# New offsets in the time table of a fused attention and MLP kernel

## Chip, cores and metric

The kernel runs on one core of one Trainium2 chip. The metric is the device time of one execution in microseconds; below that is 1107.98 us, the median of three runs (1107.72 to 1108.46).

## The reference

```python
qn = q / (np.linalg.norm(q, axis=1, keepdims=True) + 1e-06)      # q, k, v: (2, 6016, 256)
kn = k / (np.linalg.norm(k, axis=1, keepdims=True) + 1e-06)
s = kn.transpose(0, 2, 1) @ qn / tau
s = s - s.max(-1, keepdims=True)
a = np.exp(s)
a /= a.sum(-1, keepdims=True) + 1e-09
x = (v @ a).reshape(12032, 256)
h = x @ w_in                                                       # (256, 2048)
g = np.maximum(h, 0.0) + alpha * np.minimum(h, 0.0)
return g @ w_out                                                   # (2048, 256)
```

For each of two batches a 256 x 256 attention matrix is made over channels. It is multiplied into v, and the result goes through a two-layer MLP of hidden width 2048 with a leaky activation of a slope per hidden unit.

## The kernel before

The attention matrix and the first weight matrix are multiplied together once per batch (the blocks M), so the long part is only v @ M, the activation, and a product with w_out. The tokens are cut into 24 tiles (12 per batch) of 504 or 500, and the hidden width into eight pairs of 128, so there are 192 items, numbered tile x 8 + pair. All products are done in three passes of split fp32r operands (a high and a low part; `passes`, L486 to L488). Each item's first product is done as seven small block products in place of eight, so that TensorE saves an eighth and VectorE and ScalarE add and copy more.

The stages of an item i, each a planned step:

- `pe_a` (TensorE): two block products into bank q (six matmuls of half a tile's width). `copies` (ScalarE, L1015, L1016): they are copied into the accumulators r and into p7.
- `pe_b` (two products), then the *sum* `add_p7(i, 0)` (VectorE, L1032): r0 + p7 is written into bank r1. `pe_c` (two products) may come only behind it, since it adds to both. Then the second sum `add_p7(i, 1)`, and behind it `pe_d` (one product).
- `act_n` (ScalarE, L1045) multiplies by the slope, and the *maximum* `dve_g` (VectorE, L1054) makes g out of r and that. Both exist for fi = 0 and 1. The maximum of fi = 1 reads bank r1. In most tiles the next item has the same bank r1, so `add_p7(i+1, 0)` must wait until `dve_g(i, 1)` has finished reading it, though both run on VectorE.
- g is split by `g_high` (ScalarE, L1063) and `g_low` (VectorE, L1067), and `s2_first` and `s2_second` (TensorE) multiply by w_out into banks X. In 18 of the tiles, for four or six items of eight, the second product is done with seven blocks as well. There `g_sums` (VectorE, L1126, three chained differences into t), `x_high`, `x_low`, `t_high` (ScalarE, L1154) and `t_low` take the place of `g_high` and `g_low`. `t_low` is an ACTIVATE on ScalarE (L1148, the negative of a high part) and then an *adding transfer* that GpSimd issues (L1149), a DMA that adds t to it in place. `s2_second` of the item needs it from its second matmul on. The tiles g and t share a ring of four buffers, so a late adding transfer also holds back a later `act_n`.
- Per tile, `combine` and `finish_out` (L1230, L1236, L1242) put the output together and store it. `v_sums`, `v_high` and `v_low` prepare the next tile of v (L701, L719, L727). Behind `v_low(t, 0)` SP issues the load of the tile after it (`load_v`, L683), since there is one buffer. In the first batch `load_T` (L754) reads q and k once more for the norms of the second batch.

The first 92 us are written out by hand: the scores of batch 0, its softmax, and M. From there on all 4,051 steps come from a plan. Each has a slot (5.0 apart, one per item), a place within the slot from `ORDER` or a similar table, and an offset from `MOVED`, by stretch and slot. The sum of the three is its time, and the steps are issued in the order of these times. So only the order counts, and each engine's queue gets its steps in that order. The stretches are "first" (slots 0 to 20), "early" (from 21, and from 80; its eight offsets repeat per tile), "soft" (from 66), "m1" (from 90), "late" (from 108; repeats per tile for ten tiles) and "last" (from 188). For "early" the places are those of "sums" in slots whose item minus 2 takes the seven-block form (pe_b 2.29, s2 1.53 and 4.71, add 3.9, dve_g 4.3 and 2.85, g_sums 0.02, 0.2 and 2.04), and else those of "none" (pe_a 0.3, pe_c 0.7). In slot i stand pe_a, copies, pe_b and the first sum of item i, but pe_c, the second sum, pe_d, act_n and dve_g of item i - 1, and x, t and g parts of item i - 2.

```python
key = stretch(i) + (f.__name__ + "_".join(str(a) for a in args[1:]),)
time = i * PERIOD + at + MOVED.get(key[:2], {}).get(key[2], 0.0)
plan.append((time, len(plan), key, f, args))
...
for _, _, _, f, args in sorted(plan, key=lambda x: x[:2]):
    f(*args)
```

Of the kernel before, what the change touches and what calls it, by code (L numbers as in the profile page):

```python
# [79 lines left out]
    ("first", 3): dict(act_n0=-1.0, act_n1=-0.1, add_p70=1.5, add_p71=0.77, conv_b=0.8,  # L80
        copies=0.57, dve_g0=2.73, dve_g1=5.09, g_high0=0.59, g_high1=1.18, g_low0=4.24,
        g_low1=4.96, pe_a=-2.37, pe_b=0.2, pe_c=-0.27, pe_d=-0.64, pe_fill=1.89, pe_s2=-0.69,
        split_wo=2.74),
    ("first", 4): dict(act_n0=1.1, act_n1=0.17, add_p70=-0.93, add_p71=1.05, copies=0.47,
        dve_g0=1.01, dve_g1=0.84, g_high0=1.33, g_high1=2.64, g_low0=1.1, g_low1=2.99,
        pe_a=-2.16, pe_b=-1.38, pe_c=0.93, pe_d=-0.11, pe_s2=-0.28, split_wo=-2.54, v_high1=7.05,
        v_sums0=-3.0, v_sums1=0.98),
    ("first", 5): dict(act_n0=0.04, act_n1=4.41, add_p70=-0.69, add_p71=-0.69, copies=-0.77,
        dve_g0=-0.01, dve_g1=5.92, g_high1=-1.47, g_low0=2.1, g_low1=-1.59, load_T0=-2.8,
        load_T1=-3.28, load_T2=6.67, pe_a=-3.81, pe_b=-1.96, pe_c=-1.52, pe_d=-2.56, pe_s2=-1.46,  # L90
        square_T0=-2.45, square_T1=1.36, square_T2=2.03, v_high0=-2.49, v_high2=2.11),
    ("first", 6): dict(act_n0=0.21, act_n1=0.07, add_p70=0.12, copies=0.8, dve_g0=0.5,
        dve_g1=0.91, g_high0=-0.8, g_high1=2.49, g_low0=-0.85, g_low1=3.36, pe_a=-1.75,
        pe_b=-1.15, pe_c=-2.65, pe_d=-1.8, pe_s2=-0.69, v_low0=-0.41),
    ("first", 7): dict(act_n0=-1.63, act_n1=-1.7, add_p70=0.18, add_p71=-0.75, copies=-0.74,
        dve_g0=-1.2, dve_g1=-0.39, g_high0=-1.05, g_high1=-2.52, g_low0=-0.12, g_low1=-3.0,
        pe_a=-1.61, pe_b=-0.72, pe_c=-0.92, pe_d=-2.05, pe_s2=-0.73, v_low1=3.87, v_low2=-3.11),
    ("first", 8): dict(act_n0=-0.48, act_n1=2.35, add_p70=0.17, add_p71=-0.17, copies=2.22,
        dve_g0=-0.3, dve_g1=1.48, evac=6.09, g_high0=3.97, g_high1=-3.21, g_low0=3.66,
        g_low1=-0.62, pe_a=-2.57, pe_b=0.46, pe_c=-1.18, pe_d=0.57, pe_s2=-0.51),  # L100
    ("first", 9): dict(act_n0=-2.31, act_n1=0.63, add_p70=-0.18, add_p71=-0.38, copies=1.48,
        dve_g0=0.96, dve_g1=0.54, g_high0=-0.89, g_high1=-0.37, g_low0=0.56, g_low1=-2.28,
        pe_a=-0.57, pe_b=0.03, pe_c=-1.85, pe_d=-2.31, pe_s2=-0.91, s_weights0=-13.67,
        s_weights1=-3.96, s_weights2=-3.42, s_weights3=-8.36, s_weights4=4.64, v_sums0=-2.21,
        v_sums1=4.9),
    ("first", 10): dict(act_n0=0.1, act_n1=2.33, add_p70=0.54, add_p71=1.08, copies=0.84,
        dve_g0=0.18, dve_g1=1.73, g_high0=3.94, g_high1=-0.61, g_low0=3.4, g_low1=-2.19,
        pe_a=-1.46, pe_b=-0.91, pe_c=-1.87, pe_d=0.88, pe_s2=0.27, s_weights0=-10.6,
        s_weights1=-0.09, s_weights2=1.29, s_weights3=-1.45, s_weights4=3.57,
        s_weights_high=4.86, v_high0=-3.62, v_high1=2.17, v_high2=0.26),  # L110
    ("first", 11): dict(act_n0=0.59, act_n1=0.06, add_p70=1.28, add_p71=-0.62, copies=0.7,
        dve_g0=0.7, dve_g1=1.33, g_high0=6.9, g_high1=1.24, g_low0=6.07, g_low1=-1.19, pe_a=0.06,
        pe_b=1.9, pe_c=-1.26, pe_d=-1.73, s2_first=-3.59, s_weights0=-5.95, s_weights1=-2.47,
        s_weights2=-0.94, s_weights3=-4.51, s_weights4=5.66, s_weights_high=3.08,
        s_weights_low=6.86),
    ("first", 12): dict(act_n0=-0.09, act_n1=1.67, add_p70=-0.11, add_p71=-0.12, copies=0.32,
        dve_g0=0.6, dve_g1=0.85, g_high0=5.03, g_high1=0.44, g_low0=5.09, g_low1=3.0, pe_a=-0.2,
# [1485 lines left out]
```

## Time and profile before

| | |
|---|---|
| median of three runs | 1107.98 us |
| profiled execution | 1108.53 us, its span 1106.8 us |
| TensorE busy | 1098.9 us (99%) |
| weight loads busy | 1026.3 us (93%) |
| VectorE, ScalarE busy | 967.8 us (87%), 904.0 us (82%) |
| GpSimd busy | 127.5 us (12%) |

TensorE's matmuls and its weight loads have rows of their own (PE and PEld). A load normally runs under the matmul ahead of it. A matmul that must wait for a semaphore holds its load back as well, so such waits stand with PEld. DVE is VectorE, ACT ScalarE, POOL GpSimd, SP the queue of most loads and stores.

### The profile page before, as it was taken

Reading aid. Unit: us, or ns where it says so; the run is one execution under the profiler, and the core shown is the slowest. Engines: PE = TensorE matmul, PEld = TensorE weight load, DVE = VectorE, ACT = ScalarE, POOL = GpSimd, SP = SyncE. Lnnn points to the kernel's source line nnn. Section 1 sums busy time; section 2 is a strip of 40 time slices with the busy share of each in tenths; the row PEclk is TensorE's granted clock in tenths of the full one; section 3 lists DMA queues with packets and bytes.
Section 4 is the critical chain, followed back from the end, with each engine's and each line's share of the span. In section 5 each row is a group of like instructions: output and inputs, shape, how many; then the busy total and the mean of one; then the engine's idle time right before and its main releaser. Section 6 shows DMA issues by size and latency. Waiting matters only on the chain.

```text
span 1106.8 us, 20835 instructions
## 1 busy us (share of the span) xinstructions
PE 1098.9 (99%) x7752; PEld 1026.3 (93%) x7752; DVE 967.8 (87%) x1853; ACT 904.0 (82%) x1553; POOL 127.5 (12%) x156
## 2 busy tenths in 40 slices
PE   9999999999999999999999999999999999999998
PEld 8888888999999899899999989999999999999997
DVE  6798898888888888988988988999999999999975
ACT  6797777888888789777777778889889889888965
POOL 0000000011011011011000001121211122112100
PEclk9999999999999999999999999999999999999999
DMA  9997322545545545123431207557667666666520
GB/s 329 374 332 277 79 74 73 138 113 124 136 114 124 131 113 130 38 74 76 94 97 46 63 8 157 121 116 147 132 116 139 130 126 131 129 128 131 112 57 19
DMA packets 68661, 139.69 MB, mean 126 GB/s; under 512 B 6224, under 2 KB 37200, under 8 KB 68432
## 3 DMA queue, kind: packets, MB, share of 16 engines
q0 software_dynamic: 31040, 64.15, 31.1%
q1 hardware_dynamic: 37520, 74.21, 19.7%
q8 instruction: 61, 1.00, 0.4%
q14 instruction: 40, 0.33, 0.1%
HBM read 59.78 MB, written 14.42 MB: 67 GB/s over the span
## 4 chain that ended last, share of the span: by engine, by line
PE 94%; DMA 2%; DVE 2%; ACT 1%; issue 0%; SPq 0%; ACTq 0%; DVEq 0%
PE X L486 13%; PE X L487 13%; PE X L488 13%; PE r L486 11%; PE r L488 10%; PE r L487 10%; PE S L788 7%; PE o L1270 4%; PE q L488 4%; PE q L486 4%; PE q L487 4%; DMA tgl<-t 1%; PE pm L940 1%; DVE g L1054 1%; ACT g L1045 0%; DMA kqs<-q_dram 0%
## 5 line engine op out<-in xcount | busy, mean ns | idle before, releaser
L1054 DVE SCALAR_TENSOR_TENSOR g<-r,sgn,g 128x500 f32<-128x500 f32 (+1 forms) x384 | 280.4, 735 | 44.9 <-ACT g L1045 42.3
L1045 ACT ACTIVATE g<-r,salpha 128x500 f32<-128x500 f32 (+1 forms) x384 | 258.3, 681 | 58.3 <-DVE r L1032 19.9
L486 PE MATMUL r<-vs,m 128*128 128x250 f32 (+1 forms) x960 | 276.1, 288 | 2.0 <-DVE r L1032 1.6
L487 PE MATMUL r<-vs,m 128*128 128x250 f32 (+1 forms) x960 | 268.1, 279 | 0.0
L488 PE MATMUL r<-vs,m 128*128 128x250 f32 (+1 forms) x960 | 268.1, 279 | 0.0
L486 PEld LDWEIGHTS r<-vs,m 128*128 128x128 f32 x960 | 180.8, 188 | 20.2 <-DVE r L1032 8.3
L1032 DVE TENSOR_TENSOR r<-r,p 128x250 f32<-128x250 f32 (+1 forms) x384 | 162.5, 423 | 41.3 <-PE r L488 26.2
L487 PEld LDWEIGHTS r<-vs,m 128*128 128x128 f32 x960 | 181.3, 189 | 6.0
L488 PEld LDWEIGHTS r<-vs,m 128*128 128x128 f32 x960 | 181.6, 189 | 0.0
L1015 ACT COPY r<-q 128x500 f32<-128x500 f32 (+1 forms) x192 | 109.1, 568 | 76.0 <-DVE g L1054 43.9
L1149 POOL DMA_DIRECT2D tgl<-t x92 | 79.2, 861 | 572.9 <-ACT tgl L1148 422.0
L1067 DVE TENSOR_TENSOR gl<-g,gh 128x500 fp32r<-128x500 f32 (+1 forms) x200 | 133.0, 673 | 13.7 <-ACT gh L1063 13.5
L1063 ACT CAST gh<-g 128x500 fp32r<-128x500 f32 (+1 forms) x200 | 120.1, 613 | 27.7 <-DVE g L1054 24.5
L486 PE MATMUL X<-gh,wo 128*128 128x500 f32 (+1 forms) x336 | 131.6, 392 | 0.0
L487 PE MATMUL X<-gl,wo 128*128 128x500 f32 (+1 forms) x336 | 131.4, 391 | 0.0
L488 PE MATMUL X<-gh,wo 128*128 128x500 f32 (+1 forms) x336 | 131.2, 391 | 0.0
L486 PE MATMUL q<-vs,m 128*128 128x250 f32 (+1 forms) x384 | 107.6, 280 | 0.0
L488 PE MATMUL q<-vs,m 128*128 128x250 f32 (+1 forms) x384 | 107.2, 279 | 0.0
L487 PE MATMUL q<-vs,m 128*128 128x250 f32 (+1 forms) x384 | 107.2, 279 | 0.0
L1148 ACT ACTIVATE tgl<-t 128x1000 fp32r<-128x1000 f32 (+1 forms) x92 | 95.7, 1040 | 0.8 <-DVE t L1126 0.7
L1154 ACT CAST tgh<-t 128x1000 fp32r<-128x1000 f32 (+1 forms) x92 | 94.1, 1035 | 0.0
L1135 DVE TENSOR_TENSOR xl<-g,xh 128x750 fp32r<-128x750 f32 (+1 forms) x92 | 85.8, 932 | 0.0
(142 smaller groups left out, 2443.0 us busy)
## 6 DMA issues: line engine op xcount, KB each, us to landing
tgl<-t POOLq DMA_DIRECT2D x66, 500.0 KB, 4.6
tgl<-t POOLq DMA_DIRECT2D x26, 504.0 KB, 4.6
kqT<-kqT_dram SPq DMA_DIRECT2D x20, 512.0 KB, 3.7
kq<-k_dram SPq DMA_DIRECT2D x39, 256.0 KB, 5.4
kq<-q_dram SPq DMA_DIRECT2D x39, 256.0 KB, 5.4
...
```

The source lines that it names most:

```text
L486: nc.tensor.matmul(out, wh, xh, start=first, stop=False, **s)
L487: nc.tensor.matmul(out, wh, xl, start=False, stop=False, **s)
L488: nc.tensor.matmul(out, wl, xh, start=False, stop=last, **s)
L1015: nc.scalar.copy(r_t[i][0][:, :, :h], x[:, 0:1, :h].broadcast_to([P, 2, h]))
L1032: nc.vector.tensor_tensor(out=r[1][:, n, :h], in0=r[0][:, 1, :h], in1=p7_t[i][:, :h], op=ALU.add)
L1045: nc.scalar.activation(blocks(g_t[i], i, 2 * fi, 2 * fi + 2), r_t[i][fi][:, :, : half_of(i)], AF.Copy, scale=salpha[:, f : f + 1],)
L1054: nc.vector.scalar_tensor_tensor(out=g, in0=r_t[i][fi][:, :, : half_of(i)], scalar=sgn[:, f : f + 1], in1=g, op0=ALU.mult, op1=ALU.max,)
L1063: nc.scalar.copy(gs_t[i][0][:, fi, :w], g_t[i][:, fi * w : fi * w + w])
L1067: nc.vector.tensor_tensor(out=gs_t[i][1][:, fi, :w], in0=g_t[i][:, fi * w : fi * w + w], in1=f32(gs_t[i][0][:, fi, :w]), op=ALU.subtract,)
L1135: nc.vector.tensor_tensor(out=xs_t[i][1][:, h : 4 * h], in0=g_t[i][:, h : 4 * h], in1=f32(xs_t[i][0][:, h : 4 * h]), op=ALU.subtract,)
L1148: nc.scalar.activation(ts_t[i][1][:, :w], tt_t[i][:, :w], AF.Copy, scale=-1.0)
L1154: nc.scalar.copy(ts_t[i][0][:, :w], tt_t[i][:, :w])
```

## The change

Only the table `MOVED` is changed: nearly all offsets are new. No step is added or left out, no function, tile size, buffer or bank differs. On VectorE 1,156 of 1,700 instructions of the plan stand in another place of its queue, on ScalarE 864 of 1,410, on TensorE 454 of 1,169 steps, on GpSimd 9 of 148, on SP 5 of 100.

```diff
 MOVED = {
...
-    ("early", 0): dict(act_n0=-0.19, act_n1=0.14, add_p70=-1.0, add_p71=-0.14, copies=-0.55,
-        dve_g0=-1.09, dve_g1=-0.24, g_sums0=0.76, g_sums1=0.6, g_sums2=0.36, pe_a=0.4,
-        pe_b=-0.09, pe_c=0.06, pe_d=-1.12, s2_first=0.49, s2_second=-0.76, t_high=1.32,
-        t_low=2.24, v_sums0=-2.11, x_high=0.25, x_low=1.13),
+    ("early", 0): dict(act_n0=-0.21, act_n1=-0.06, add_p70=-0.43, add_p71=0.67, copies=-0.29,
+        dve_g0=-0.9, dve_g1=-0.28, g_sums0=1.59, g_sums1=2.36, g_sums2=0.86, pe_a=-0.5,
+        pe_b=-0.1, pe_c=0.07, pe_d=-1.43, s2_first=0.89, s2_second=-0.75, t_high=-1.04,
+        t_low=1.81, v_sums0=0.77, x_high=0.41, x_low=2.76),
...
-    ("early", 2): dict(act_n0=0.66, act_n1=1.6, add_p70=0.2, add_p71=1.78, combine0=-1.74,
-        combine1=-0.73, combine2=0.7, combine_copy=-1.56, copies=-1.77, dve_g0=0.82, dve_g1=0.82,
-        g_sums0=-1.84, g_sums1=1.24, g_sums2=1.04, pe_a=-2.26, pe_b=1.3, pe_c=-1.18, pe_d=-0.3,
-        s2_first=-1.92, s2_second=0.61, t_high=0.15, t_low=0.91, v_high0=-11.47, x_high=1.03,
-        x_low=4.51),
-    ("early", 3): dict(act_n0=-3.17, act_n1=0.05, add_p70=0.19, add_p71=-0.19, copies=0.41,
-        dve_g0=-0.4, dve_g1=0.24, finish_out0=0.68, finish_out1=0.9, g_high0=0.48, g_high1=2.6,
-        g_low0=0.46, g_low1=5.94, pe_a=-0.28, pe_b=-2.1, pe_c=-0.3, pe_d=-1.88, s2_first=0.38,
-        s2_second=-0.52),
-    ("early", 4): dict(act_n0=1.74, act_n1=-0.03, add_p70=0.44, add_p71=0.46, copies=-2.13,
-        dve_g0=1.14, dve_g1=0.95, g_sums0=-1.05, g_sums1=0.11, g_sums2=0.29, pe_a=-3.12,
-        pe_b=1.45, pe_c=-1.19, pe_d=0.65, s2_first=0.29, s2_second=-1.66, t_low=2.8, v_low0=0.31,
-        x_high=0.39, x_low=2.3),
+    ("early", 2): dict(act_n0=1.15, act_n1=0.52, add_p70=0.56, add_p71=0.47, combine0=0.16,
+        combine1=0.21, combine2=0.49, combine_copy=-0.13, copies=0.3, dve_g0=0.29, dve_g1=0.87,
+        g_sums0=-1.3, g_sums1=1.19, g_sums2=0.7, pe_a=-2.0, pe_b=1.18, pe_c=-2.05, pe_d=0.36,
+        s2_first=-0.27, s2_second=-0.87, t_high=-0.07, t_low=2.97, v_high0=-10.75, x_high=1.01,
+        x_low=2.55),
+    ("early", 3): dict(act_n0=-1.76, act_n1=0.18, add_p70=-0.56, add_p71=-0.28, copies=0.43,
+        dve_g0=-1.17, dve_g1=0.21, finish_out0=-0.66, finish_out1=-0.78, g_high0=0.3,
+        g_high1=0.07, g_low0=8.08, g_low1=5.25, pe_a=-0.81, pe_b=-1.43, pe_c=-1.13, pe_d=-1.65,
+        s2_first=-1.33, s2_second=-0.48),
+    ("early", 4): dict(act_n0=2.88, act_n1=1.1, add_p70=-0.55, add_p71=-1.43, copies=1.24,
+        dve_g0=1.8, dve_g1=0.17, g_sums0=-1.14, g_sums1=2.85, g_sums2=1.5, pe_a=-1.6, pe_b=0.58,
+        pe_c=-1.82, pe_d=2.75, s2_first=2.62, s2_second=-2.61, t_high=-1.55, t_low=3.47,
+        v_low0=3.42, x_high=-1.02, x_low=4.54),
...
-        load_T0=-0.91, load_T1=-2.11, load_T2=1.54, pe_a=-1.54, pe_b=-0.83, pe_c=-0.7, pe_d=0.38,
+        load_T0=-2.31, load_T1=3.68, load_T2=1.61, pe_a=-0.25, pe_b=-0.7, pe_c=0.16, pe_d=-0.47,
...
-    ("late", 0): dict(act_n0=0.12, act_n1=1.46, add_p71=0.83, copies=0.55, dve_g0=-0.3,
-        dve_g1=0.97, g_sums0=1.27, g_sums1=1.1, g_sums2=0.01, pe_a=-3.1, pe_b=1.52, pe_c=-0.47,
-        pe_d=-0.54, s2_first=-3.25, s2_second=2.69, t_high=-3.55, t_low=0.55, v_sums0=-4.53,
-        x_high=1.21, x_low=-0.28),
+    ("late", 0): dict(act_n0=0.01, act_n1=1.46, add_p70=0.29, add_p71=-0.75, copies=0.94,
+        dve_g0=-0.12, dve_g1=1.25, g_sums0=1.14, g_sums1=1.06, g_sums2=-0.66, pe_a=-1.78,
+        pe_b=0.56, pe_c=-0.77, pe_d=-0.29, s2_first=-4.77, s2_second=2.23, t_high=-4.33,
+        t_low=0.61, v_sums0=-5.14, x_high=1.78, x_low=1.88),
...
-    ("late", 3): dict(act_n0=-0.14, act_n1=-0.31, add_p70=0.03, add_p71=0.26, copies=-0.22,
-        dve_g0=-0.08, dve_g1=0.65, finish_out0=1.11, finish_out1=0.1, g_high0=1.02,
-        g_high1=-0.82, g_low0=2.17, g_low1=-1.4, g_sums0=0.36, g_sums1=2.3, g_sums2=1.05,
-        pe_a=-1.08, pe_b=0.01, pe_c=-1.1, pe_d=-0.92, pe_s2=0.8, s2_first=-2.29, s2_second=-1.74,
-        t_high=-0.16, t_low=1.03, x_high=2.18, x_low=1.88),
+    ("late", 3): dict(act_n0=-0.96, act_n1=0.04, add_p70=0.27, add_p71=0.28, copies=-1.87,
+        dve_g0=-0.13, dve_g1=0.03, finish_out0=-0.63, finish_out1=-0.25, g_high0=-1.36,
+        g_high1=-0.88, g_low0=-0.47, g_low1=2.26, g_sums0=-0.44, g_sums1=0.42, g_sums2=-0.06,
+        pe_a=-2.49, pe_b=-0.07, pe_c=-0.66, pe_d=-1.57, pe_s2=-0.83, s2_first=-0.38,
+        s2_second=-0.57, t_high=-4.75, t_low=0.12, x_high=0.19, x_low=1.95),
...
 }
```

## Rows read from the trace of the kernel before

**Rows 1.** The page, busy time of each engine, share of span, instructions.

```profile
PE 1098.9 (99%) x7752; PEld 1026.3 (93%) x7752; DVE 967.8 (87%) x1853; ACT 904.0 (82%) x1553; POOL 127.5 (12%) x156
```

**Rows 2.** Busy time by stretch, from the column heads on.

```profile
core 0: us, PE busy (x) PEld busy (x) DVE busy (x) ACT busy (x) POOL busy (x), PEclk, DMA share, GB/s
...
201.00:437.00 236.00, 234.18 (x1693) 218.19 (x1693) 208.16 (x391) 198.70 (x349) 28.52 (x35) 1.00 0.52 126
...
667.00:1070.00 403.00, 402.96 (x3184) 390.12 (x3183) 369.62 (x700) 357.63 (x580) 76.66 (x87) 1.00 0.63 126
```

**Rows 3.** Waits of the weight loader, 201 to 437 us: total, times, longest.

```profile
PEld r L486 <- DVE r L1032: 3.5, 13, 0.7
PEld X L487 <- DMA tgl<-t: 1.5, 2, 1.3
PEld X L486 <- ACT tgh L1154: 0.5, 3, 0.2
PEld r L486 <- ACT r L1015: 0.4, 1, 0.4
```

**Rows 4.** Waits of the weight loader, 91 to 201 us.

```profile
PEld r L486 <- DVE r L1032: 1.2, 3, 0.7
PEld r L486 <- ACT r L1015: 1.1, 3, 0.4
PEld o L1270 <- DVE gl L1067: 0.4, 2, 0.2
```

**Rows 5.** Waits of the weight loader for sums, 437 to 562 us.

```profile
PEld r L486 <- DVE r L1032: 1.0, 2, 0.5
```

**Rows 6.** Waits of the weight loader for sums, 562 to 667 us.

```profile
PEld r L486 <- DVE r L1032: 0.4, 1, 0.4
```

**Rows 7.** Waits of the weight loader, 667 to 1070 us.

```profile
PEld r L486 <- DVE r L1032: 2.2, 11, 0.3
```

**Rows 8.** Timeline of TensorE at a sum of item 32: start, us, engine, line.

```profile
264.49 0.28 PE L487 MATMUL q<-vs,m 128*128 128x250 f32 x1
264.61 0.28 PE L488 MATMUL q<-vs,m 128*128 128x250 f32 x1
264.86 0.38 PE L486 MATMUL r<-vs,m 128*128 128x250 f32 x1
265.08 0.28 PE L487 MATMUL r<-vs,m 128*128 128x250 f32 x1
```

**Rows 9.** Timeline of VectorE at the same sum.

```profile
263.53 0.74 DVE L1054 SCALAR_TENSOR_TENSOR g<-r,sgn,g 128x504 f32<-128x504 f32 x1
264.37 0.43 DVE L1032 TENSOR_TENSOR r<-r,p 128x250 f32<-128x250 f32 x1
264.71 0.73 DVE L1054 SCALAR_TENSOR_TENSOR g<-r,sgn,g 128x504 f32<-128x504 f32 x1
```

**Rows 10.** Timeline of GpSimd, the adding transfer of item 50.

```profile
371.42 0.88 POOL L1149 DMA_DIRECT2D tgl<-t  x1 [11.10 <-PE r L488]
```

**Rows 11.** Timeline of SP, the load of v beside it.

```profile
371.78 0.39 SPq L683 DMA_DIRECT2D v<-vT_dram  x1
```

**Rows 12.** Timeline of TensorE, the matmul that waits for that transfer.

```profile
379.67 0.39 PE L487 MATMUL X<-tgl,ws 128*128 128x250 f32 x1 [1.05 <-DMA tgl<-t]
```

**Rows 13.** Tile tgl, 201 to 437 us: from issue to landing of its transfers.

```profile
DMA to landing us min/median/max: 4.5/4.6/8.2
```

**Rows 14.** The same, 667 to 1070 us.

```profile
DMA to landing us min/median/max: 4.5/4.6/6.2
```

**Rows 15.** Timeline of ScalarE, its part of t_low of item 137.

```profile
829.33 1.03 ACT L1148 ACTIVATE tgl<-t 128x1000 fp32r<-128x1000 f32 x1
```

**Rows 16.** Timeline of GpSimd, the adding transfer of that item.

```profile
830.67 0.85 POOL L1149 DMA_DIRECT2D tgl<-t  x1 [4.04 <-ACT tgl L1148]
```

**Rows 17.** Timeline of TensorE, the first matmul that uses it.

```profile
836.88 0.28 PE L487 MATMUL X<-tgl,ws 128*128 128x250 f32 x1
```

More of the change, by code (lines that the diff above doesn't have):

```diff
@@ L80 @@
[L80 to L117, printed above, removed]
-        pe_b=-2.29, pe_c=-0.6, pe_d=-1.95, s2_first=3.31, s2_second=-0.94, s_weights_high=10.96,
-        s_weights_low=-3.03, v_low0=1.93),
@@ L359 @@
-    ("late", 7): dict(act_n0=0.29, act_n1=1.85, add_p70=0.74, add_p71=-2.26, copies=-0.16,
-        dve_g0=0.29, dve_g1=1.77, g_sums0=2.41, g_sums1=2.4, g_sums2=0.86, pe_a=-3.02,
-        pe_b=-0.05, pe_c=-2.97, pe_d=-1.09, s2_first=-2.59, s2_second=0.73, t_high=-1.68,
-        t_low=2.11, x_high=1.28, x_low=0.57),
-    ("last", 0): dict(act_n0=1.06, act_n1=2.64, add_p70=1.01, add_p71=1.41, copies=-2.62,
-        dve_g0=1.12, dve_g1=2.71, g_high0=-2.17, g_high1=1.86, g_low0=3.13, g_low1=3.33,
-        pe_a=-3.8, pe_b=-0.7, pe_c=0.39, pe_d=-0.18, pe_s2=-0.8),
@@ new lines @@
+    ("first", 18): dict(act_n0=0.44, act_n1=1.11, add_p70=-0.49, add_p71=0.32, copies=1.12,
+        dve_g0=-0.56, dve_g1=0.5, g_sums0=1.04, g_sums1=0.95, g_sums2=-0.13, pe_a=0.73,
+        pe_b=0.65, pe_c=0.43, pe_d=-0.16, s2_first=-3.57, s2_second=1.81, t_high=2.94,
+        t_low=1.09, v_high0=10.44, x_high=1.82, x_low=1.24),
+    ("first", 19): dict(act_n0=-1.0, act_n1=0.28, add_p70=2.18, add_p71=-0.87, copies=-1.65,
+        dve_g0=1.84, dve_g1=1.93, finish_out0=-0.56, finish_out1=2.92, g_high0=0.93,
+        g_high1=-0.95, g_low0=2.48, g_low1=-2.58, pe_a=-1.97, pe_b=-1.7, pe_c=-2.01, pe_d=-2.23,
+        s2_first=-0.48, s2_second=-2.69),
@@ new lines @@
+    ("late", 3): dict(act_n0=-0.96, act_n1=0.04, add_p70=0.27, add_p71=0.28, copies=-1.87,
[3 more added lines that the diff above has]
+        s2_second=-0.57, t_high=-4.75, t_low=0.12, x_high=0.19, x_low=1.95),
+    ("late", 4): dict(act_n0=0.04, act_n1=-0.05, add_p70=0.49, add_p71=0.27, copies=-1.83,
+        dve_g0=0.61, dve_g1=1.53, g_sums0=-0.57, g_sums1=-0.09, g_sums2=1.02, pe_a=-2.22,
+        pe_b=1.05, pe_c=-0.04, pe_d=-0.83, s2_first=-1.37, s2_second=-0.08, t_high=1.8,
+        t_low=0.46, v_low0=0.74, x_high=-1.14, x_low=1.79),
@@ new lines @@
+    ("late", 5): dict(act_n0=-2.62, act_n1=-0.08, add_p70=-1.74, add_p71=-0.26, copies=0.2,
+        dve_g0=-2.35, dve_g1=-0.74, g_high0=1.1, g_high1=0.08, g_low0=1.45, g_low1=-2.39,
+        pe_a=-3.09, pe_b=-1.56, pe_c=-0.31, pe_d=-1.38, s2_first=-2.4, s2_second=-0.03,
+        v_add=1.16, v_minus=-0.09),
+    ("late", 6): dict(act_n0=-1.9, act_n1=-2.38, add_p70=-2.82, add_p71=-2.09, copies=-2.2,
+        dve_g0=-1.36, dve_g1=-3.3, g_sums0=-0.69, g_sums1=-0.21, g_sums2=-0.94, pe_a=-3.07,
+        pe_b=-2.37, pe_c=-3.65, pe_d=-2.31, s2_first=2.54, s2_second=-1.8, t_high=-0.45,
+        t_low=-0.83, x_high=0.06, x_low=0.59),
@@ new lines @@
+    ("late", 7): dict(act_n0=0.5, act_n1=-0.18, add_p70=0.29, add_p71=-0.83, copies=-0.02,
+        dve_g0=0.52, dve_g1=0.44, g_sums0=-1.65, g_sums1=1.53, g_sums2=-0.27, pe_a=-3.83,
+        pe_b=1.12, pe_c=-4.15, pe_d=-0.19, s2_first=-2.34, s2_second=3.34, t_high=-3.54,
+        t_low=0.35, x_high=0.67, x_low=-0.56),
+    ("last", 0): dict(act_n0=1.26, act_n1=2.36, add_p70=1.14, add_p71=1.21, copies=0.17,
+        dve_g0=1.8, dve_g1=3.25, g_high0=3.25, g_high1=1.82, g_low0=3.05, g_low1=3.09,
+        pe_a=-4.78, pe_b=0.46, pe_c=0.97, pe_d=-0.79, pe_s2=-0.14),
```

491 lines of the change are left out of this document (256 added, 235 removed).

## Prediction

> **What bounds the kernel now.** I read the page's busy times first, then the same by stretch, then who TensorE and its weight loader wait for, then the instructions around typical waits. TensorE is busy for 1098.9 us of the 1106.8 us span [rows 1], so nothing shortens the kernel but the removal of TensorE's own waits. By stretch [rows 2] TensorE is full in all three and its granted clock is 1.00 (2.4 GHz); VectorE is at 88% (201 to 437 us: 208.16 of 236) and 92% (667 to 1070 us: 369.62 of 403), ScalarE at 84% and 89%. They don't bound by their totals, but a backlog on VectorE makes a sum come late, and TensorE then waits for that sum. The waits stand with the weight loader, because a matmul that must wait holds back its weight load first. The view of its waits shows 3.5 us in 13 waits for the sums (L1032) between 201 and 437 us, 1.5 us in two waits for an adding transfer, 0.5 and 0.4 us for ScalarE [rows 3]; 2.7 us between 91 and 201 us [rows 4]; 1.0 us and 0.4 us for sums in the next two stretches [rows 5, 6]; 2.2 us in 11 waits between 667 and 1070 us, about one per tile [rows 7]. Sum: 5.9 + 2.7 + 1.0 + 0.4 + 2.2 = 12.2 us. That is the whole prize; the rest of the span is matmuls, whose number stays.
>
> What one such wait costs: undisturbed, one matmul of this width follows the other after 0.12 us (264.49 to 264.61); the next one, which waits for a sum, starts at 264.86 and the one behind it at 265.08 [rows 8]. So the wait costs 0.25 + 0.22 - 2 x 0.12 = 0.23 us; the second half is a weight load that nothing covers any more. The loader's 3.5 / 13 = 0.27 us agrees, so I use the loader's rows as TensorE's loss.
>
> **The change part by part.** It gives 4,051 planned steps new offsets and adds, removes or resizes no instruction. What follows is counted from the two tables by the kernel's own formula (slot x 5 + place + offset, sorted).
>
> 1. *pe_b to pe_c.* The first sum of an item (add_p7 n=0) reads what pe_b leaves and pe_c may start only behind it. Item 50 before: pe_b at 250 + 2.29 + 1.30 = 253.59, pe_a of item 51 at 255.02, pe_c at 255.40: only six matmuls of 0.12 us, 0.7 us, cover the sum. After: 253.47, s2_first of 47 at 254.44, pe_a at 254.49, pe_c at 254.57: six matmuls of 500 columns more. Steps with only a pe_a between were 21 and are 0 (12 of them in items 21 to 65, the 201 to 437 stretch); the least cover is now nine matmuls, 1.05 us. The wait at 264.86 [rows 8] is such a step (item 32). A sum takes 0.43 us [rows 9], and with its two hand-overs it overran six matmuls by 0.13 us there (0.25 - 0.12), so nine are enough if VectorE is free. The other kind in that stretch is item 5 of each tile, where the sum is late in VectorE's queue. There two v_low and a g_low leave the queue ahead of the sum, and one x_low comes in. I take 3.0 of 3.5 us; ends 0 and 3.5.
>
> 2. *Other work between a maximum and a sum.* Maximum (dve_g, L1054) of item 31 at 263.53 for 0.74 us, sum at 264.37, next maximum at 264.71 [rows 9]. The sum starts 0.10 us after the maximum ends; the instruction behind the sum starts 0.09 us before the sum ends. So a sum that reuses the maximum's bank right behind it costs VectorE 0.19 us more than another instruction in that place. Example: item 48's sum before at 240 + 3.9 - 1.0 = 242.90, right behind dve_g(47,1) at 242.61; after, g_sums at 242.90 and dve_g(47,0) at 243.40 stand between, the sum at 243.47. Such direct pairs fall from 134 to 87 (40 to 17 in items 21 to 65, 59 to 49 in items 108 to 187): 47 x 0.19 = 8.9 us of VectorE time, which TensorE sees only where VectorE is backlogged: in the last stretch, and at item 5 above. In the last stretch one pair and two chained g_sums per tile lose their neighbour, a g_low leaves the run ahead of item 4's sum, and item 1's second sum goes ahead of the last g_sums. I take 1.6 of 2.2 us; ends 0 and 2.2.
>
> The Trainium skill (VectorE: DVE Perf Modes, section The DRAIN you can't avoid) says against this that every VectorE operation is followed by a pipeline flush and that "the semaphore costs nothing extra here"; by that, part 2 is worth 0. The trace of before disagrees: the 0.10 us gap and the 0.09 us overlap stand side by side.
>
> 3. *Loads against adding transfers.* At 371.42 GpSimd issues an adding transfer, at 371.78 SP issues the load of v [rows 10, 11]. TensorE stood 1.05 us for it, at 379.67 [rows 12]. Adding transfers take 4.6 us in the median and up to 8.2 us in this stretch [rows 13]. The load is issued behind a v_low that goes from 265.50 to 268.61, while the adding transfer's step goes from 265.46 to 266.13: the load now starts 2.5 us behind it, not with it, and the next load_T goes from 270.39 to 276.18. There it can meet the following adding transfer, whose buffer is wanted sooner than before. I take 1.3 of 1.5 us; ends +1.0 (it merely moves to the next transfer) and -1.5.
>
> 4. *The rest.* ScalarE's hand-overs (0.9 us in the 201 stretch) -0.3; the start (2.7 us, where most steps move and the same short cover occurs three times) -1.0 of 2.7; -0.8 of 1.0 and -0.3 of 0.4 in the two middle stretches, where six of the 21 short covers lie.
>
> 5. *What it costs.* TensorE has the same matmuls in another order: nothing. 1,156 of 1,700 VectorE places and 864 of 1,410 ScalarE places change, so new waits will appear that no row shows. Below: none. Above: as many as the 26 waits for sums of [rows 3, 5, 7] together, 6.7 us. I take seven, 7 x 0.23 = +1.6 us. One is visible: per tile of the last stretch the adding transfer of item 1 now stands behind t_high (a copy of the same shape as ScalarE's part of it, 1.03 us [rows 15]), and that of item 6 behind act_n and t_high. Before, GpSimd issues it at 830.67 [rows 16] and TensorE uses it at 836.88 [rows 17]: 6.21 us for a transfer of 4.6 us, at most 6.2 [rows 14]. About 0.9 us later leaves 0.7 us of slack: enough for 4.6, not for 6.2. Estimate from the median and the maximum: two of the nine of item 1 and two of item 6 lose some 0.3 us each: 4 x 0.3 = +1.2 us. Ends 0 and rival C.
>
> Sum: -3.0 - 1.6 - 1.3 - 0.3 - 1.0 - 0.8 - 0.3 = -8.3; +1.6 + 1.2 = +2.8; net -5.5 us. The profiled execution took 1108.53 us (span 1106.8 and 1.7 around it), so 1103.0 us; it lies 0.55 above the median of 1107.98, so the forecast of the median is 1102.5 us.
>
> **Rivals.** A: *nearly all waits go* (short covers gone, VectorE ahead everywhere, no new ones): 1108.0 - 11 = 1097. For it: the 1.05 us cover; against: two thirds of VectorE's places change, with 8% of its time free in the last stretch. Chance 0.14. B: *a new wait for each old one*: ScalarE (89%) or VectorE becomes late elsewhere, net gain 1 us: 1107. For it: VectorE's 92% in the last stretch; against: 8.9 us less of its time is spent. Chance 0.15. C: *the later adding transfers decide*, the other side: items 1 and 6 of nine tiles of the last stretch, 18 transfers, each issued 0.9 to 1.5 us later, hold TensorE. At 6.2 us each the wait is 0.8 us and the next weight load 0.1: 18 x 0.9 = +16 us, so 1108 - 8.3 + 16 = 1116. It decides once the mean over the 18 passes 8.3 / 18 = 0.46 us, that is transfers of some 5.8 us in the mean; the median of 4.6 speaks against. Chance 0.09, at about 1111. D: *the distance between maximum and sum saves VectorE nothing* (what the section named above would make of it): parts 2 and the item 5 share fall away, 1.6 + 0.9 + 0.5 of the start, 1102.5 + 3.0 = 1105.5. The gap and overlap of [rows 9] speak against. Chance 0.05.
>
> **How the numbers follow.** The forecast has 0.57. What this kernel's measurement can tell is about 0.2%, 2.2 us: forecast, A and D are faster (0.76), B the same (0.15), C slower (0.09). The range for 8 in 10 leaves out C and the outermost part of A: 1097 to 1107.6.
>
> **What would show it.** Right: in the profile after, waits of the weight loader for sums fall from 8 us to some 3 us, with hardly any at pe_c between 201 and 437 us; TensorE's 1 us stop for an adding transfer is gone; the direct maximum-sum gaps of 0.10 us are fewer; span near 1101. Wrong: adding transfers at the head of the loader's waits between 667 and 1070 us (C), ScalarE's r copies or sums in new places with the old total (B), or fewer 0.10 us gaps with the same waits for sums (D).

## The result and the profile after

| | before | after |
|---|---|---|
| median beside each other, first time | 1108.18 us (1107.72 to 1108.46) | 1097.69 us (1096.05 to 1098.51) |
| the same, once more (e9 below) | 1108.69 us (1107.6 to 1109.5) | 1096.15 us (1094.73 to 1098.6) |
| profiled execution | 1108.53 us, span 1106.8 | 1098.51 us, span 1096.7 |

The ratio is 0.9904 with a 95% interval of 0.9887 to 0.9921 the first time, 0.989 (0.9877 to 0.9903) the second: faster by 1.0%. The forecast was 1102.5 us in a range of 1097.0 to 1107.6. The sign is right and the first median lies within the range, but the gain of 10.5 us is nearly twice the 5.5 us forecast, and the second median lies just below the range. The time is that of rival A, 1097; its mechanism (nearly all waits go, no new ones come) is not what happened, as the count by items below shows.

The diff adds one line ahead of the kernel's code, so L1032 of before is L1033 of after, and so on. The page's busy times, to set beside [rows 1]:

```profile
PE 1087.6 (99%) x7752; PEld 1023.2 (93%) x7752; DVE 962.0 (88%) x1853; ACT 909.4 (83%) x1553; POOL 127.8 (12%) x156
```

TensorE has the same 7,752 matmuls and is busy 11.3 us less, which is more than the whole gain. The recorded times of matmuls overlap (0.28 us each, started 0.12 us apart in [rows 8]), so a wait of up to 0.16 us leaves no idle time, and the matmul that waited there is recorded with 0.38 us. Three groups of the page make that visible; the columns are busy time, mean ns of one, and idle time ahead of it with what ended most of it. Before:

```profile
L486 PE MATMUL r<-vs,m 128*128 128x250 f32 (+1 forms) x960 | 276.1, 288 | 2.0 <-DVE r L1032 1.6
L486 PEld LDWEIGHTS r<-vs,m 128*128 128x128 f32 x960 | 180.8, 188 | 20.2 <-DVE r L1032 8.3
L1032 DVE TENSOR_TENSOR r<-r,p 128x250 f32<-128x250 f32 (+1 forms) x384 | 162.5, 423 | 41.3 <-PE r L488 26.2
```

After:

```profile
L487 PE MATMUL r<-vs,m 128*128 128x250 f32 (+1 forms) x960 | 270.1, 281 | 0.7 <-DVE r L1033 0.7
L487 PEld LDWEIGHTS r<-vs,m 128*128 128x128 f32 x960 | 180.9, 188 | 10.0 <-DVE r L1033 3.0
L1033 DVE TENSOR_TENSOR r<-r,p 128x250 f32<-128x250 f32 (+1 forms) x384 | 162.3, 423 | 54.5 <-PE r L489 44.7
```

Read the three together. The first matmul of a product into r takes 281 ns in place of 288, the loader's idle time ahead of it halves from 20.2 to 10.0 us, and the part of it named for the sums falls from 8.3 to 3.0 us. The last line of each is the other side of it: ahead of its sums VectorE now stands 44.7 us, not 26.2, until TensorE's product is there. The sums come ahead of TensorE, where before TensorE often came ahead of them.

The loader's waits of after in the stretch from 201 to 437 us [rows 3 of before], and then from 667 to 1070 us [rows 7]: total, times, longest.

```profile
PEld r L487 <- DVE r L1033: 1.6, 3, 1.1
```

```profile
PEld X L488 <- DMA tgl<-t: 3.2, 4, 1.0
PEld r L487 <- DVE r L1033: 0.2, 1, 0.2
```

In the first stretch 13 waits for sums are three, and those for adding transfers and ScalarE are gone. In the last stretch 11 waits for sums are one, and four waits for an adding transfer, which were none, are new. In the same two stretches of [rows 2] the busy times of after are:

```profile
core 0: us, PE busy (x) PEld busy (x) DVE busy (x) ACT busy (x) POOL busy (x), PEclk, DMA share, GB/s
...
201.00:437.00 236.00, 235.33 (x1745) 223.10 (x1745) 208.62 (x401) 205.53 (x357) 28.71 (x35) 1.00 0.53 128
...
667.00:1070.00 403.00, 400.60 (x3166) 388.61 (x3166) 367.66 (x699) 356.46 (x577) 75.05 (x85) 1.00 0.62 123
```

In the first window TensorE does 52 matmuls more in the same 236 us (1745 for 1693); in the last, 18 fewer, since a window at fixed times holds other items now. So I also counted by items: for each matmul of a trace, how much later than undisturbed (the usual distance of two matmuls of these widths) it starts behind the one ahead of it, where that is over 20 ns, summed. (us; the second execution of after is that of e9 below.)

| items | before | after | after again |
|---|---|---|---|
| by hand, ahead of item 0 | 2.06 | 2.87 | 1.79 |
| 0 to 20 | 3.79 | 2.58 | 2.60 |
| 21 to 65 | 7.63 | 1.52 | 0.98 |
| 66 to 89 | 2.31 | 0.32 | 0.33 |
| 90 to 107 | 1.18 | 0.10 | 0.10 |
| 108 to 187 | 4.18 | 4.10 | 2.18 |
| sum | 21.15 | 11.5 | 8.0 |

The sums differ by 9.7 us between the first two, and their spans by 10.1: this is where the time came from. More than half of the loss of before is still there in the first execution of after, 11.5 of 21.15 us. So rival A's 1097 us came true by luck: the loss was larger than the 12.2 us that the forecast and its rivals start from, and a smaller part of it went.

The sum of item 32 is the one of [rows 8, 9]. TensorE after (start, us, engine, line):

```profile
264.89 0.39 PE L488 MATMUL X<-gl,wo 128*128 128x504 f32 x1
265.12 0.39 PE L489 MATMUL X<-gh,wo 128*128 128x504 f32 x1
265.36 0.28 PE L487 MATMUL r<-vs,m 128*128 128x250 f32 x1
265.47 0.28 PE L488 MATMUL r<-vs,m 128*128 128x250 f32 x1
```

VectorE after, at the same sum:

```profile
263.09 0.74 DVE L1055 SCALAR_TENSOR_TENSOR g<-r,sgn,g 128x504 f32<-128x504 f32 x1
263.75 0.41 DVE L1127 TENSOR_TENSOR t<-g,t 128x252 f32<-128x252 f32 x1
264.07 0.74 DVE L1055 SCALAR_TENSOR_TENSOR g<-r,sgn,g 128x504 f32<-128x504 f32 x1
264.73 0.42 DVE L1033 TENSOR_TENSOR r<-r,p 128x250 f32<-128x250 f32 x1
265.05 0.94 DVE L1136 TENSOR_TENSOR xl<-g,xh 128x756 fp32r<-128x756 f32 x1
```

Matmuls of 504 columns (s2_first) stand ahead of pe_c, the sum ends at 264.73 + 0.42 = 265.15, and pe_c starts at 265.36 without a wait. Between the maximum that read the bank (263.09) and the sum stand two other instructions, and each of the last four starts 0.08 to 0.10 us ahead of the end of the one before it.

One new wait of the last stretch, item 129: GpSimd issues the adding transfer, and TensorE's first matmul that uses it. The bracket gives the idle time ahead and what ended it.

```profile
781.07 0.85 POOL L1150 DMA_DIRECT2D tgl<-t  x1 [5.00 <-ACT tgl L1149]
```

```profile
786.03 0.28 PE L487 MATMUL X<-tgh,ws 128*128 128x250 f32 x1
786.93 0.38 PE L488 MATMUL X<-tgl,ws 128*128 128x250 f32 x1 [0.62 <-DMA tgl<-t]
787.14 0.28 PE L489 MATMUL X<-tgh,ws 128*128 128x250 f32 x1
```

Before, item 137 had 6.21 us from issue to use [rows 16, 17]. Here TensorE would have been there at 786.15, 5.08 us behind the issue, and the transfer took 5.8. This is rival C's mechanism, at four of 18 transfers.

### The profile page after: what moved, and what is told of

It is laid out like the page before. It is cut to its first block, busy times and chain, and to the rows that moved or that the text cites. A ratio compares the mean times of both kernels' runs of the same rounds, so it can differ in the third digit from the quotient of the medians.

```text
span 1096.7 us, 20812 instructions
## 1 busy us (share of the span) xinstructions
PE 1087.6 (99%) x7752; PEld 1023.2 (93%) x7752; DVE 962.0 (88%) x1853; ACT 909.4 (83%) x1553; POOL 127.8 (12%) x156
## 4 chain that ended last, share of the span: by engine, by line
PE 88%; DMA 4%; DVE 4%; issue 2%; ACT 1%; SPq 0%; POOLq 0%; DVEq 0%; ACTq 0%
PE X L488 13%; PE X L487 13%; PE X L489 13%; PE r L487 9%; PE r L489 9%; PE r L488 9%; PE S L789 5%; PE o L1271 4%; PE q L487 4%; PE q L488 4%; PE q L489 4%; DMA tgl<-t 3%; DMA v<-vT_dram 1%; DVE g L1055 1%; DMA kqs<-q_dram 1%
## 5 line engine op out<-in xcount | busy, mean ns | idle before, releaser
L1033 DVE TENSOR_TENSOR r<-r,p 128x250 f32<-128x250 f32 (+1 forms) x384 | 162.3, 423 | 54.5 <-PE r L489 44.7
L1132 ACT CAST xh<-g 128x750 fp32r<-128x750 f32 (+1 forms) x92 | 76.2, 829 | 18.8 <-DVE g L1055 18.8
```

What stands on the lines that cost most here:

```text
L1033: nc.vector.tensor_tensor(out=r[1][:, n, :h], in0=r[0][:, 1, :h], in1=p7_t[i][:, :h], op=ALU.add)
```

## The experiments

All kernels were timed beside the kernel before on the same chip; in brackets the 95% interval of the ratio to it. "By items" means the count of the table above.

**e1_low_first**: the kernel after, t_low of item 1 put ahead of its t_high.

```diff
-    ("late", 3): dict(... t_high=-4.75, t_low=0.12, ...)
+    ("late", 3): dict(... t_high=-4.75, t_low=-0.2, ...)
```

> The changed kernel with one offset altered: in each tile of the last stretch t_low of item 1 goes ahead of t_high, so that its adding transfer is issued about 1 us sooner. Theory (the later issue is what lets slow transfers of 5.6 to 5.8 us hold TensorE, four times, 3.2 us in the loader's waits): the four waits vanish, 1097.7 - 3.1 = 1094.6 us. Rival (the transfer is slow because it meets something at a fixed time, and an earlier one meets something else): waits of the same total elsewhere, 1097 to 1098 us.

Measured: 1094.1 us (1093.71 to 1094.28), ratio 0.9875 (0.986 to 0.989). The loader's waits from 667 to 1070 us:

```profile
PEld X L488 <- DMA tgl<-t: 0.6, 1, 0.6
PEld r L487 <- DVE r L1033: 0.2, 1, 0.2
```

Four waits are one, at item 6 of a tile, and the stretch falls from 4.10 us by items (2.18 in the second execution of after) to 1.29. The four transfers of item 1 still took 5.1, 5.8, 5.1 and 5.2 us; they had more time. A copy of 1.03 us in ScalarE's queue had cost that; nothing waited for the copy in its later place.

**e2_cover_alone**: the kernel before, only TensorE's order changed, so that s2_first covers the sum in place of pe_a alone.

```diff
-    ("early", 0): dict(... s2_first=0.49, ...)      ("early", 2): dict(... s2_first=-1.92, ...)
+    ("early", 0): dict(... s2_first=-1.7, ...)      ("early", 2): dict(... s2_first=0.4, ...)
```

> The kernel before with part 1 alone: in the early stretches s2_first goes between pe_b and pe_c of items 0 and 2 of each tile, so that 12 to 15 covers of six matmuls get six matmuls of 500 columns more. Theory (the cover alone makes these waits): they go, 2.9 us in TensorE's steps, 1105.3 us. Rival (VectorE is late there anyway, the waits move to pe_d or to the next item): 1107.5 to 1108.5 us.

Measured: 1116.62 us, ratio 1.0079 (1.0065 to 1.0093): slower by 8.5 us, against both theories. TensorE at item 32:

```profile
268.09 0.28 PE L487 MATMUL r<-vs,m 128*128 128x250 f32 x1
268.21 0.28 PE L488 MATMUL r<-vs,m 128*128 128x250 f32 x1
269.01 0.38 PE L486 MATMUL r<-vs,m 128*128 128x250 f32 x1 [0.52 <-DVE r L1032]
269.23 0.28 PE L487 MATMUL r<-vs,m 128*128 128x250 f32 x1
```

pe_c's waits at items 0 and 2 of the tiles are gone, but s2_first had been the cover of the *second* sum, and now pe_d of item 0 follows pe_c directly: 269.01 - 268.21 - 0.12 = 0.68 us and 0.10 us more, in each tile. At pe_d of item 1 the same happens in six tiles, with some 0.7 us and 0.10 more (1.07 at item 49). The loader's waits for sums from 201 to 437 us go from 3.5 us in 13 to 10.1 us in 17. TensorE's work to put over sums was taken from one sum, and was missing at the next.

**e3_load_alone**: the kernel before, the load of v a planned step of its own, 3.0 later in the plan.

```diff
-        if part == 0 and t:
-            vloads.done("vraw")
+    def v_next(t):
+        vloads.done("vraw")
```

> The kernel before with part 3 alone: the load of v is released by a step of its own 3 planned us behind v_low, for the tiles whose load met the adding transfer of item 2; VectorE's order is untouched. Theory (the load beside it makes that transfer slow): these transfers fall from 5.9 to 8.2 us to about 5 us, TensorE's 1.05 us stop and the two waits of 0.5 us four items later go, 2.4 us, 1105.8 us. Rival (other transfers make it slow, or the later load holds v up): 1108 us or more.

Measured: 1107.58 us, ratio 0.9994 (0.9985 to 1.0003). The test failed as a test. GpSimd's adding transfer of item 50 and SP's load:

```profile
371.04 0.87 POOL L1149 DMA_DIRECT2D tgl<-t  x1 [11.09 <-ACT tgl L1148]
```

```profile
371.41 0.39 SPq L683 DMA_DIRECT2D v<-vT_dram  x1
```

They are 0.37 us apart, as in [rows 10, 11]. In the plan a step's time orders a queue and nothing else; SP's queue had nothing to put ahead of the load, so it left as soon as v_low had released the buffer. Only a later v_low moves it. e11 was made for what this one missed.

**e4_early_alone**: the kernel before with the eight "early" rows of after.

```diff
-    ("early", 0): dict(...), ... ("early", 7): dict(...),   # as before
+    ("early", 0): dict(...), ... ("early", 7): dict(...),   # as after
```

> The kernel before with the new offsets of the stretch named early alone (slots 21 to 65 and 80 to 89). Theory (the waits that go lie in this stretch: 7.6 us of them become 1.5, and about 1 us in slots 80 to 89): 1101 us. Rival (the gain is spread over all stretches, and the new order meets the old one badly at its two ends): 1104 to 1106 us.

Measured: 1103.41 us, ratio 0.9959 (0.9946 to 0.9971), so -4.7 us. By items the stretch itself falls from 7.63 to 1.24 us. Two new waits of 0.78 us stand at pe_d of items 65 and 89, where the new order meets the old one: a part of the gain is lost at a joint that was made for other neighbours. Elsewhere 0.6 us came back at item 13, whose pe_b waits for ScalarE, and 0.4 at the adding transfer of item 145. Item 13's loss ranges from 0.46 us (before) to 1.06 (here) in the seven profiled executions that have this order there, so that part is variation.

**e5_cover_j0**: the kernel before, one step of TensorE moved that pe_d does not need.

```diff
-    ("early", 1): dict(... s2_second=-0.46, ...)
+    ("early", 1): dict(... s2_second=-3.29, ...)
```

> The kernel before with one offset changed: s2_second of the item three back (slot 1 of the early table, -0.46 to -3.29) now stands between pe_a and pe_c of item 0 of each tile (items 24, 32, ..., 88) in place of behind s2_first. pe_d keeps s2_first as its cover, and no other engine's queue changes. Theory (short covers cost a wait each; a cover that nobody else needs is free): the waits of these pe_c in the trace of before (0.26, 0.24, 0.23, 0.21, 0.21, 0.22 and, in the soft stretch, 0.13 and 0.09 us) go, 1.6 us in all: 1106.5 us against 1108.1. Rival (covers are zero-sum: the sum of item 0 is late by VectorE's order, and whoever stands next waits instead, or s2_second waits for its own g): the time stays, 1107.9 to 1108.5.

Measured: 1109.19 us, ratio 1.0013 (1.0004 to 1.0021). The theory missed; others wait instead, as the rival had it, and the time is above its range too. The waits of item 0 are gone in all eight tiles (0.21 to 0.26 us each in six of them). In six tiles a later s2_second (items 22, 30, 38, 46, 54 and 78), which TensorE now reaches sooner, waits for ScalarE's `combine_copy` (L1214) from the bank that it adds to: 0.17 to 0.21 us each, 1.2 us in all. And two new waits stand at items 65 and 89, where the next stretch's order begins:

```profile
438.85 0.38 PE L486 MATMUL r<-vs,m 128*128 128x250 f32 x1 [0.53 <-DVE r L1032]
```

Each loses 0.80 us where it lost 0.08. The same step had stood between pe_d of item 64 and pe_b of item 65; without it TensorE comes sooner to a sum that hangs on VectorE's unchanged queue. By items this execution lost 1.5 us more than before, 1.1 of it ahead of item 0, which this edit does not touch: the edit itself gave nothing and cost little.

**e6_late_alone**: the kernel before with the eight "late" rows of after, edited as in e4.

> The kernel before with only the eight offsets' rows of the last stretch taken from the kernel after (the late table, items 108 to 187). Theory: in this stretch the change gives nothing, since the sums' waits that it takes away (4.2 us by the matmuls' start times of before, 0.6 after) come back as waits for the adding transfer of item 1 in every second tile (0.6 to 1.0 us, four of them, with the steps behind them 3.5 us): 1107.6 us, between 1107 and 1109 with what the joint to the old order costs. Rival (the forecast's own terms, 1.6 gained and 1.2 lost in all, half of the loss being here): 1106.9 or less. Rival (this stretch carries a good part of the 10.5 us): 1104 to 1105.

Measured: 1105.84 us, ratio 0.998 (0.9971 to 0.9989), so -2.1 us: between the theories. By items the stretch goes from 4.18 to 2.10 us. The waits for sums are all but gone (0.19 us left), as expected; the adding transfers took back 1.9 us and not 3.5, at two tiles and not four. That difference led to e9.

**e7_cover_undone**: the kernel after with the short cover put back at item 2 of six tiles; VectorE's new order stays.

```diff
-    ("early", 2): dict(... s2_first=-0.27, ...)
+    ("early", 2): dict(... s2_first=0.0, ...)
```

> The kernel after with one offset changed: s2_first of the item three back (slot 2 of the early table, -0.27 to 0.0) goes back behind pe_c, so that only a pe_a stands between pe_b and pe_c of item 2 of each tile (items 26, 34, 42, 50, 58, 82), as in the kernel before; VectorE's new order stays. In the kernel after the sum ends 1.21 to 1.43 us before that pe_c, and the work taken away is 1.40 us long. Theory (the cover is what took these waits away, and the loader's second half of 0.10 us comes with every wait): waits of 0.15 to 0.35 us in five of the six places, +1.3 us: 1099.0 us. Rival (VectorE's new order alone took them away): 1097.7 us, no wait there.

Measured: 1095.99 us, ratio 0.9891 (0.9876 to 0.9906). TensorE at item 34:

```profile
273.35 0.28 PE L488 MATMUL q<-vs,m 128*128 128x250 f32 x1
273.46 0.28 PE L489 MATMUL q<-vs,m 128*128 128x250 f32 x1
273.78 0.38 PE L487 MATMUL r<-vs,m 128*128 128x250 f32 x1
273.99 0.28 PE L488 MATMUL r<-vs,m 128*128 128x250 f32 x1
```

The waits came back where and as large as expected: 0.20, 0.30, 0.31, 0.18, 0.18 and 0.09 us at items 26, 34, 42, 50, 58 and 82, 1.26 us in all. The time did not rise, since in the profiled execution the last stretch lost only 1.40 us by items in place of 4.10, with one wait for an adding transfer. By items 21 to 65 it lost 2.3 us, and after 1.5 and 1.0. At the place the theory holds; the time of the whole kernel can't tell it, because something else varies more (after itself took 1094.73 to 1098.6 us).

**e8_pair_back**: e1 with two VectorE steps of the last stretch back in the old neighbourhood. (In one item of 192, item 186, the first sum then stands ahead of pe_b and lacks its product.)

```diff
-    ("late", 2): dict(... add_p70=0.56, ...)      ("late", 3): dict(... add_p71=0.28, ...)
+    ("late", 2): dict(... add_p70=0.0, ...)       ("late", 3): dict(... add_p71=-0.315, ...)
```

> The kernel after with item 1's t_low ahead of its t_high (as in e1_low_first, 1094.1 us against 1108.1 of before), and two offsets of VectorE in the last stretch put back as in the kernel before: the sum of item 2 stands again directly behind the maximum that reads its bank (0.56 to 0.0 in slot 2), and the second sum of item 2 no longer stands between two chained g_sums (0.28 to -0.315 in slot 3). Nothing is added, and TensorE's, ScalarE's and the DMA queues are as they were. Theory (a dependent neighbour on VectorE costs 0.19 us more than a separated one, a chained difference 0.12, so item 4's sum, which ends 0.28 us before its pe_c, comes too late): a wait of some 0.2 us at item 4 of each of ten tiles, +1.8 us: 1095.9 us. Rival D of the forecast (distance between the two saves nothing, since VectorE must empty anyway): 1094.1 us, item 4 does not wait.

Measured: 1100.14 us, ratio 0.993 (0.9917 to 0.9942): 6.0 us above e1, three times the expected loss. By items the stretch goes from 1.29 to 6.68 us: per tile 0.27 at item 3, 0.25 at item 4, and some 0.05 to 0.1 at item 3's pe_d. VectorE at item 122's sum:

```profile
731.26 0.74 DVE L1055 SCALAR_TENSOR_TENSOR g<-r,sgn,g 128x504 f32<-128x504 f32 x1
732.44 0.43 DVE L1033 TENSOR_TENSOR r<-r,p 128x252 f32<-128x252 f32 x1 [0.44 <-PE r L489]
```

The sum waits for more than the maximum: VectorE stands 0.44 us until pe_b's product is there (0.36 to 0.50 in nine tiles). In the kernel after two other instructions fill that time. In the kernel before, the same pair stands in the queue so much later than pe_b that this wait does not exist; VectorE at item 122:

```profile
743.09 0.74 DVE L1054 SCALAR_TENSOR_TENSOR g<-r,sgn,g 128x504 f32<-128x504 f32 x1
743.93 0.43 DVE L1032 TENSOR_TENSOR r<-r,p 128x252 f32<-128x252 f32 x1
```

So e8 loses by a wait that its own order makes, larger than the 0.19 us that I had priced, and it does not measure what the change gained here. Rival D's time for this edit is missed by 6.0 us, but since a wait that D says nothing of is in that number, the 0.19 us of a direct neighbour is not tested alone.

**e9_after_again**: the kernel after, unchanged.

> The kernel after, unchanged, once more beside the kernels below. In its first profile item 1's adding transfer of every second tile of the last stretch took 5.6 to 5.8 us and TensorE waited for it four times (3.2 us); in two other kernels with the same order there (cover_undone, late_alone) the same four took 5.7, 4.8, 4.6, 5.0 and 5.8, 4.8, 5.7, 4.5 us and one or two waits were left. Theory (how long these transfers take changes from execution to execution, the order only sets how much slack they have): 1096 to 1098 us, with one to four of the four waits. Rival (the order fixes them): 1097.7 us with the same four waits.

Measured: 1096.15 us (1094.73 to 1098.6). The loader's waits from 667 to 1070 us:

```profile
PEld X L488 <- DMA tgl<-t: 1.4, 2, 1.0
PEld r L487 <- DVE r L1033: 0.2, 1, 0.2
```

Two of the four waits, at items 113 and 129; at 145 and 161 the same transfers took 4.5 us in place of 5.8. The order sets how much time there is, and each execution sets how much is needed. Of the 3.8 us between the two profiled executions of this kernel (1098.51 and 1094.73) the last stretch makes 1.9 by items and the work ahead of item 0 1.1.

**e10_ring_shift**: the kernel after; the ring of g and t is moved on by two buffers at item 106.

```diff
+            if i == 106:
+                for n in range(2):
+                    skip = rnpool.tile([P, 2 * TW], F32, tag="rn", name=f"skip{n}")
+                    nc.scalar.copy(skip[:, :2], sgn[:, :2])
```

> The kernel after with two more tiles taken once, at item 106, from the ring of four buffers that g and t share (two elements are copied into each, so nothing is computed differently). A tile of the last stretch takes 14 buffers of this ring, so item 1's t stands in the same two buffers in every second tile; the two extra ones exchange the halves from there on. Theory (the slow transfers belong to a place in the ring): the slow ones move from items 113, 129, 145, 161 to items 121, 137, 153, 169, same time within 1 us. Rival (they belong to something else that alternates, as the buffers of v): the slow ones stay at 113, 129, 145, 161.

Measured: 1100.19 us, ratio 0.9922 (0.9909 to 0.9935). The transfers of items 113, 129, 145 and 161 took 5.7, 5.2, 5.7 and 5.3 us, those of 121, 137, 153 and 169 took 4.5 to 4.7: they stayed. The place in this ring is not what makes them slow. The kernel lost 7.58 us by items in the last stretch. 2.9 us of that stand beside the edit, at items 104, 107 and 108, where the two buffers are taken; six waits for transfers make 3.8 us by the loader's view, two of them at item 6. Why the edit raises these too is open, as is what does alternate from tile to tile.

**e11_no_load**: the kernel before without the loads of v from the fourth tile on; the later tiles compute with the third tile's raw v.

```diff
+        if t > 2:
+            v_raw[t] = v_raw[t - 1]
+            return
```

> The kernel before without the loads of v from the fourth tile on: each later tile computes with the raw v of the third, so 21 transfers of 500 KB are gone and nothing else (the output is that of other data). It is the upper end of what moving these loads can give, since e3_load_alone did not move them in time. Theory (part 3 of the forecast, a load beside an adding transfer makes it late): the adding transfers of item 2 in the early stretch fall from 6 to 8 us to 4.5 to 5, the waits for them there (1.5 us by the loader, 1.05 by the matmuls) go: 1106 us. Rival (the transfer is late for another reason, or the loads' waits are not what TensorE waits for): 1107.5 to 1108.3 us.

Measured: 1104.71 us (1104.06 to 1107.05; a seventh execution, of 2773.28 us, is not counted in the ratio), ratio 0.9969 (0.9958 to 0.9981): 4.0 us faster than before. The loader's waits from 201 to 437 us [rows 3 of before], and the adding transfers there from issue to landing [rows 13]:

```profile
PEld r L486 <- DVE r L1035: 1.8, 10, 0.2
PEld r L486 <- ACT r L1018: 0.4, 1, 0.4
PEld X L486 <- ACT tgh L1157: 0.2, 1, 0.2
```

```profile
DMA to landing us min/median/max: 4.5/4.6/6.3
```

By items the stretch falls from 7.63 to 4.03 us, by 3.6: the waits for transfers, and also waits for *sums*, which TensorE's rows don't connect with a load, above all pe_d of items 38 and 54 (0.52 us each, now none) and pe_c of item 50 (0.50, now 0.16). They stand four items behind the slow transfers of items 34 (7.1 us) and 50 (8.2 us), or at one of them. Transfers of item 2 now take 4.5 to 5.6 us. Not every slow transfer goes: that of item 40 still takes 6.3 us.

The rows of the other engines make the connection. In the kernel before, ScalarE's act_n of item 37 needs a buffer that the adding transfer of item 34 still reads, VectorE's maximum waits for act_n, and the second sum of item 38, queued behind it, comes late for pe_d:

```profile
295.24 0.68 ACT L1045 ACTIVATE g<-r,salpha 128x500 f32<-128x500 f32 x1 [1.60 <-DMA tgl<-t]
295.95 0.74 DVE L1054 SCALAR_TENSOR_TENSOR g<-r,sgn,g 128x500 f32<-128x500 f32 x1 [0.90 <-ACT g L1045]
299.88 0.39 PE L486 MATMUL r<-vs,m 128*128 128x250 f32 x1 [0.25 <-DVE r L1032]
```

ScalarE's waits for adding transfers in the whole kernel, before and then after:

```profile
ACT g L1045 <- DMA tgl<-t: 7.5, 8, 2.7
```

```profile
ACT g L1046 <- DMA tgl<-t: 2.5, 4, 1.8
```

Without the loads they are 1.9 us.

**e12_low_first2**: e1 with the same exchange at item 6.

```diff
-    ("late", 0): dict(... t_low=0.61, ...)
+    ("late", 0): dict(... t_low=0.525, ...)
```

> e1_low_first (the kernel after with item 1's t_low ahead of its t_high in the last stretch, 1094.1 us) with the same exchange at item 6 (offset of t_low in slot 0 of the late table 0.61 to 0.525, one ACTIVATE of 1.0 us earlier). In e1_low_first item 6's transfer had 0.36 us of slack and was waited for once (0.6 us). Theory: that wait goes and nothing else moves, 1093.6 us. Rival (t_high's step was the one in time to spare for x and s2, so another wait takes its place): 1094.1 to 1095 us. Both beat the kernel after beside it.

Measured: 1094.19 us (1093.46 to 1094.4), ratio 0.9869 (0.9856 to 0.9881). Item 126's wait is gone, one of 0.1 us stands at item 161: the same time as e1, and below every run of the kernel after beside it (1094.73 at least). Both versions beat the kernel before; e1 was not timed beside the kernel after.

## Why the forecast was right in sign and too small

**The prize was under-counted.** The step "so I use the loader's rows as TensorE's loss" failed. The view that names waits gave 12.2 us; the start times of the matmuls give 21.15 us, 19.1 of them in the planned part. Two things are missing in the named waits: the weight load behind a waiting matmul (0.10 us each time, which I had seen at [rows 8] but not added to the rows), and waits too short to be named. In the last stretch the view named 2.2 us in 11 [rows 7]; by items it was 4.18 us, in two waits per tile: 0.25 us at item 4 and 0.10 to 0.17 at item 1.

**Part 1, covers, -3.0.** The waits at the short covers are gone, but the step gave them the wrong worth and the wrong cause. e2 and e5 show that these covers alone gave nothing: +8.5 us, and +1.3 us of which 1.1 lie ahead of item 0, because each cover was another step's. e7 shows what it is worth together with VectorE's new order: 1.26 us at six places. And e11 shows that up to 3.6 us of this stretch hung on the loads. The stretch gave 6.1 us, so where the loads are counted first, some 2.5 us are left for covers and VectorE's order together.

**Part 2, work between, -1.6.** The waits for sums of the last stretch fell by 3.6 us by items, and e6 has the same with this stretch alone. The term was too small for the reason just given: it is 1.6 of the 2.2 us that the view named, where 4.18 were lost. Its mechanism stays argued. What I priced is there: in the kernel after, as before, a maximum's direct successor starts 0.10 us behind its end, a separated one 0.08 to 0.10 us ahead of it, and direct pairs are fewer as counted. But no run takes that price alone: e8, meant for it, made a wait for pe_b that before does not have. The Trainium skill (VectorE: DVE Perf Modes, section The DRAIN you can't avoid) has a flush behind every operation, and adds that "A next op that is not held starts earlier". The forecast left that sentence out, so the section speaks less against part 2 than it said. In the kernel after, too, the starts 0.08 to 0.10 us ahead of the end of the one before agree with that addition.

**Part 3, loads, -1.3.** The direction was right and the size was a third of what there was: e11 puts the upper end at 4.0 us. I had counted the two waits that name a transfer. But a transfer that is late also keeps its buffers, and the work behind it comes late; the waits that follow carry VectorE's name, as the rows at e11 show. In the kernel after the transfers of item 2 in this stretch take 4.5 to 5.2 us but for one (6.35 us, with the load of v and that of kqT beside it), where they took 5.9 to 8.2. That one stays as the stretch's only large wait, 0.93 us at pe_d of item 30, by the same path: where the transfer of item 26 took 6.35, 5.86, 5.70 and 5.41 us (after, e10, e9 and e12, with the same order there), pe_d of item 30 lost 0.93, 0.62, 0.46 and 0.19 us.

**Part 4, the rest.** Start -1.2 for -1.0, though at items 0 to 4 new waits (one of 0.8 us, nine of 0.19 to 0.30) stand for old ones (one of 0.8, one of 0.5, six of 0.19); the middle stretches -2.0 and -1.1 for -0.8 and -0.3.

**Part 5, the cost.** The term +1.6 for seven new waits did not appear: besides item 30 there is none above 0.2 us at items 21 to 107, with VectorE and TensorE re-ordered together. The term +1.2 for later adding transfers was the right mechanism at item 1: 3.2 us by the loader's view in the first execution, 1.4 in the second, gone with e1. Item 6 kept 0.3 us of slack. Rival C's condition, 0.46 us in the mean over 18 transfers, was not met.

By their own signs rivals B and D are out: outside items 0 to 4 no new wait came for each old one, and the waits for sums fell from 8.3 to 3.0 us by the page. What stays open is why item 1's transfer is slow in every second tile, and by how much the single parts overlap: e4 and e6 give 4.7 and 2.1 us of the 10.5, each with joints to the old order.
